# Loading k, q and v with one DMA per head pair instead of one per two head pairs

## The chip, the cores and the metric

One Trainium2 chip, one core of it. The metric is the time of one execution in microseconds on the device. Each profile is one execution taken by the hardware profiler. Runs carry a state: "slow" where a run lies over 1.5% above the fastest run of the same kernel, else "fast". With one core this is a label of spread, not of a die: the kernel before took 136.4 to 136.9 us in its first three runs.

## The reference, cut to what matters

Attention with a cosine weight (a feature map of relu times cos and sin, no softmax), whose output goes through a token mixer and a product with `w_out`:

```python
q_p = concat([relu(q) * cos, relu(q) * sin])      # also k_p; batch 8, heads 8, seq 576, head_dim 64
kv  = einsum('bhsf,bhsd->bhfd', k_p, v);  z = k_p.sum(axis=2)
x   = einsum('bhsf,bhfd->bhsd', q_p, kv) / (einsum('bhsf,bhf->bhs', q_p, z) + 1e-6)
# x: (8, 576, 512)
wq, wk = x @ w_q, x @ w_k
out = relu((wq @ wk.T / 8) @ x) @ w_out
```

All inputs and outputs are float32; q, k and v are 28 MB together and the output 9.4 MB.

## The kernel before

The kernel is one list of operations in a fixed order, each with its engine. Work goes by tile groups H = 0 to 15 (half a batch element, that is two head pairs). `LD` loads k, q or v of one group, `RK`, `CV` and `DQ` make bfloat16 of it on ScalarE, GpSimd or VectorE, `MK` multiplies k by cos and sin, `QK`, `NM`, `XT` and so on are TensorE's, and `ST` stores. All DMAs are issued by the sync engine, in the list's order.

```python
SPLIT = (0, 15)                      # groups whose loads come one head pair at a time
def part(H, s):
    return (s, s + 1) if H in SPLIT else (0, 2)

def LD(eng, pb, t, H, s):            # 54 of these; eng is the sync engine
    lo, hi = part(H, s)
    b, h = divmod(H, 2)
    eng.dma_start(raw[t][H % N_RAW][:, lo:hi, :],           # N_RAW = 5 buffers
                  srcs[t][b][:, 2 * h + lo:2 * h + hi, :])  # rows of 2,304 bytes
# ... (cut)
V.memset(warm, 1.0)
for _ in range(N_WARM):              # 14 products before the data comes
    T.matmul(bank1(7, 0, 2048, FP32), warm[:, 0:P], warm, start=True, stop=True)
```

## Time and profile before

| | before |
|---|---|
| time, first three runs | 136.85 us median (136.44 to 136.91) |
| span of the profiled execution | 136.3 us |
| busy: TensorE, VectorE, ScalarE, GpSimd | 77%, 73%, 58%, 47% |
| DMA queue of loads and stores, share of 16 engines' span | 82.0% |
| DMAs: whole loads, half loads, weights, stores | 42, 12, 3, 44 |

A busy share is an average over stages with different limits, so the digits by slice are what to read; the prediction shows them.

### The profile page before, as it was taken

The page shows a single profiled execution, that of the slowest core. Times are in us where ns is not written, and L with a number is a line of the kernel's source. Part 1 is how long each engine was busy: PE and PEld are TensorE (multiplying, and loading weights), DVE is VectorE, ACT ScalarE, POOL GpSimd, SP SyncE. Part 2 cuts the span into 40 slices and gives each one's busy share as a digit, 9 for nine tenths or more (in the row PEclk, how much of TensorE's full clock was granted, in tenths as well). Part 3 has the DMA queues.
Part 4 walks back from the last instruction along what each step waited for, and adds up shares of the span by engine and source line. Part 5 has one row for each costly group of instructions (what it writes and reads, how often), then busy time and mean ns, then how long its engine had stood idle before and what let it go on. Part 6 is the DMA issues. An engine that isn't in the chain of part 4 may idle for free.

```text
span 136.3 us, 5166 instructions
## 1 busy us (share of the span) xinstructions
PE 104.7 (77%) x2247; PEld 68.8 (50%) x2262; DVE 100.1 (73%) x180; ACT 78.9 (58%) x112; POOL 64.4 (47%) x56
## 2 busy tenths in 40 slices
PE   5932966497869859783899998999939999999600
PEld 2311955466555446553475585588514966444200
DVE  2147799988999998999279788999784697755000
ACT  7106131984878477953559957989344647434410
POOL 7635778358399947846584354434617010000000
PEclk9995599959999999999599999999995999999995
DMA  4999999999999999999999950029998461158984
GB/s 133 317 402 398 393 390 345 375 393 385 392 390 389 391 338 313 362 400 400 410 401 411 398 231 5 0 46 303 325 403 314 101 221 43 38 123 271 262 233 112
DMA packets 20070, 39.39 MB, mean 289 GB/s; under 512 B 2640, under 2 KB 2640, under 8 KB 20048
## 3 DMA queue, kind: packets, MB, share of 16 engines
q1 hardware_dynamic: 20048, 39.07, 82.0%
q8 instruction: 17, 0.28, 0.8%
q14 instruction: 5, 0.04, 0.1%
HBM read 29.62 MB, written 9.44 MB: 286 GB/s over the span
## 4 chain that ended last, share of the span: by engine, by line
PE 52%; DMA 18%; DVE 8%; issue 8%; SPq 5%; ACT 3%; POOL 1%; ACTq 0%
PE banks L400 19%; DMA vf<-in_v_dram 8%; DMA kf<-in_k_dram 7%; PE banks L279 7%; PE banks L330 6%; PE banks L247 6%; PE banks L256 4%; PE banks L313 4%; PE banks L375 3%; DMA out_dram<-osb 3%; DVE kp L219 3%; SPq L417 2%; PE banks L358 2%; SPq L195 2%; DVE xs L296 2%
## 5 line engine op out<-in xcount | busy, mean ns | idle before, releaser
L184 POOL TENSOR_SCALAR qd<-qf 128x2304 bf16<-128x2304 f32 (+1 forms) x18 | 35.3, 1964 | 13.7 <-DMA qf<-in_q_dram 10.0
L400 PE MATMUL banks<-wo_sb,mix 128*128 128x512 bf16 x129 | 35.2, 391 | 2.1 <-issue 1.6
L219 DVE TENSOR_TENSOR kp<-rk,cossin 128x2304 bf16<-128x2304 bf16 (+1 forms) x18 | 26.6, 1490 | 1.6 <-POOL rk L184 1.2
L266 DVE TENSOR_TENSOR qpt<-banks,cst 128x1152 bf16<-128x1152 bf16 x32 | 23.5, 746 | 4.7 <-PE banks L256 4.7
L174 ACT COPY osb<-banks 128x512 f32<-128x512 f32 x30 | 17.2, 589 | 14.4 <-PE banks L400 7.9
L296 DVE TENSOR_TENSOR xs<-banks,rec 128x640 bf16<-128x640 f32 x32 | 25.2, 810 | 0.2
L247 PE MATMUL banks<-vb,kp 64*128 64x65 bf16 x576 | 16.1, 197 | 9.3 <-ACT vb L174 4.5
L388 ACT ACTIVATE mix<-banks 128x640 bf16<-128x640 f32 (+1 forms) x26 | 16.8, 657 | 8.2 <-PE banks L375 8.0
L247 PEld LDWEIGHTS <-kp 64*128 64x128 bf16 x576 | 13.0, 99 | 13.7 <-DVE kp L219 6.8
L400 PEld LDWEIGHTS <-mix 128*128 128x128 bf16 x144 | 12.4, 99 | 14.2 <-issue 2.5
L279 PE MATMUL banks<-kvs,qpt 128*128 128x65 bf16 x320 | 15.8, 199 | 3.3 <-issue 1.7
L174 ACT COPY xT<-banks 128x1280 bf16<-128x1280 bf16 x11 | 13.4, 1227 | 8.0 <-PE banks L313 7.9
L279 PEld LDWEIGHTS <-qpt 128*128 128x128 bf16 x320 | 13.9, 101 | 5.5 <-DVE qpt L266 1.7
L256 PE MATMUL banks<-ident,qd 64*128 64x64 bf16 x576 | 15.1, 195 | 0.7 <-issue 0.7
L178 POOL TENSOR_SCALAR vb<-vf 128x1152 bf16<-128x1152 f32 (+1 forms) x8 | 10.0, 1256 | 11.5 <-DMA vf<-in_v_dram 8.6
L184 POOL TENSOR_SCALAR rk<-kf 128x1152 bf16<-128x1152 f32 (+1 forms) x8 | 10.1, 1267 | 10.3 <-DVE kp L219 4.9
L174 ACT CAST vb<-vf 128x1152 bf16<-128x1152 f32 (+1 forms) x10 | 11.1, 1108 | 5.4 <-DMA vf<-in_v_dram 5.4
L182 ACT ACTIVATE rk<-kf 128x1152 bf16<-128x1152 f32 (+1 forms) x9 | 10.0, 1111 | 7.2 <-DMA kf<-in_k_dram 7.2
L256 PEld LDWEIGHTS <-qd 64*128 64x128 bf16 x576 | 11.9, 98 | 0.8 <-issue 0.8
L176 DVE CAST kvs<-banks 128x130 bf16<-128x130 f32 x32 | 8.7, 279 | 4.7 <-PE banks L256 4.3
L330 PE MATMUL banks<-xT,wqk_sb 128*128 128x288 bf16 x64 | 10.2, 304 | 1.5 <-issue 1.5
L313 PE MATMUL banks<-ident,xs 64*128 64x64 bf16 x320 | 8.2, 199 | 3.8 <-issue 2.5
(50 smaller groups left out, 120.7 us busy)
## 6 DMA issues: line engine op xcount, KB each, us to landing
qf<-in_q_dram SPq DMA_DIRECT2D x14, 576.0 KB, 9.6
kf<-in_k_dram SPq DMA_DIRECT2D x14, 576.0 KB, 9.6
vf<-in_v_dram SPq DMA_DIRECT2D x14, 576.0 KB, 9.2
out_dram<-osb SPq DMA_DIRECT2D x28, 256.0 KB, 5.3
out_dram<-osb SPq DMA_DIRECT2D x16, 128.0 KB, 2.5
kf<-in_k_dram SPq DMA_DIRECT2D x4, 288.0 KB, 5.7
qf<-in_q_dram SPq DMA_DIRECT2D x4, 288.0 KB, 7.0
vf<-in_v_dram SPq DMA_DIRECT2D x4, 288.0 KB, 6.5
```

Of the source, the lines that this page charges most:

```text
L174: A.copy(dst, src)
L184: eng.tensor_scalar(dst, src, FMAX, 0.0, op0=ALU.min, op1=ALU.max)
L219: eng.tensor_mul(kp[H % N_KP][:, lo:hi], rk[H % N_RK][:, lo:hi].unsqueeze(3).to_broadcast([P, n, C9, 2, D]), cossin.unsqueeze(1).to_broadc ...
L247: T.matmul(kvp[:, hh, :], kp[H % N_KP][p0:p0 + 64, i, c, :, :], vb[H % N_VB][p0:p0 + 64, i, c, 0:D + 1], start=(c == 0), stop=(c == C9 - 1))
L256: T.transpose(qt[:, hh, c * D:(c + 1) * D], src, ident[p0:p0 + 64, p0:p0 + 64])
L266: eng.tensor_mul(qpt[g % N_QPT][:, :, 1:SLOTS, :], qk_views(at["QK", g])[0].rearrange("f h (c d) -> f h c d", c=C9), cst.unsqueeze(1).to_b ...
L279: T.matmul(nv[:, hh, u, :], qpt[g % N_QPT][:, hh, 2 * u:2 * u + 2, :], kvs[g % N_KV][:, hh, :], start=(u == 0), stop=(u == SC - 1 and not ...
L296: eng.tensor_tensor(xs[b % N_XS][:, :, 2 * pr:2 * pr + 2, :].rearrange("p u h d -> p h u d"), num_view(at["NM", g])[:, :, :, 0:D], rec[g % ...
L313: T.transpose(xv[:, r, i, u, :], xs[b % N_XS][p0:p0 + 64, u, 2 * hp:2 * hp + 2, :], ident[p0:p0 + 64, p0:p0 + 64])
L330: T.matmul(w[:, nh, :], wqk_sb[:, dmc, :], xT[b % N_XT][:, dmc, D + nh * HS:D + (nh + 1) * HS], start=(dmc == 0), stop=(dmc == NDM - 1))
L388: A.activation(dst, src, AF.Relu, scale=scale_moe)
L400: T.matmul(o, mix[b // 2 % N_MIX][:, dmc, base:base + P], wo_sb[:, dmc, :], start=(dmc == 0), stop=(dmc == NDM - 1))
```

## The change

Each load of a whole group becomes two DMAs, one per head pair, at the same place in the order. The intent is smaller pieces; no byte and no order changes.

```diff
     def LD(eng, pb, t, H, s):
         lo, hi = part(H, s)
         b, h = divmod(H, 2)
-        eng.dma_start(raw[t][H % N_RAW][:, lo:hi, :],
-                      srcs[t][b][:, 2 * h + lo:2 * h + hi, :])
+        for i in range(lo, hi):
+            eng.dma_start(raw[t][H % N_RAW][:, i, :], srcs[t][b][:, 2 * h + i, :])
```

## The prediction

> **What bounds the kernel now.** I read four views of the kernel before: the page, then the sync engine's queue in order of time, then its waits, then the waits of the compute engines on DMAs stage by stage.
>
> The page, part 2 (one digit for each 3.4 us):
>
> ```profile
> PE   5932966497869859783899998999939999999600
> ...
> DVE  2147799988999998999279788999784697755000
> ...
> DMA  4999999999999999999999950029998461158984
> GB/s 133 317 402 398 393 390 345 375 393 385 392 390 389 391 338 313 362 400 400 410 401 411 398 231 5 0 46 303 325 403 314 101 221 43 38 123 271 262 233 112
> ```
>
> The 16 DMA engines are full from 3 to 79 us at about 390 GB/s; nearly all of k, q and v arrive there. From about 65 us TensorE is full, the DMA engines are empty around 82 to 90 us, then comes a second, short load stage (to 106 us) and a tail of stores. So the first half is paced by bytes, with VectorE close behind, and the second half by TensorE. Splitting moves no bytes. It can only hurt through a cost per DMA, or through fewer bytes queued ahead.
>
> The sync engine issues all loads and stores in one order (start, duration):
>
> ```profile
> 0.73 0.40 SPq L195 DMA_DIRECT2D kf<-in_k_dram  x1
> ...
> 2.12 0.43 SPq L195 DMA_DIRECT2D qf<-in_q_dram  x1
> ...
> 8.28 0.38 SPq L195 DMA_DIRECT2D vf<-in_v_dram  x1
> 9.06 0.37 SPq L195 DMA_DIRECT2D kf<-in_k_dram  x1
> ...
> 40.91 1.26 SPq L195 DMA_DIRECT2D qf<-in_q_dram  x1
> 49.26 0.73 SPq L417 DMA_DIRECT2D out_dram<-osb  x1
> 50.03 0.58 SPq L195 DMA_DIRECT2D qf<-in_q_dram  x1
> 50.66 0.78 SPq L195 DMA_DIRECT2D vf<-in_v_dram  x1
> ...
> 89.78 0.47 SPq L417 DMA_DIRECT2D out_dram<-osb  x1
> ```
>
> Its waits (total, times, longest):
>
> ```profile
> SPq L417 <- DVE osb L176: 16.1, 2, 12.5
> SPq L417 <- ACT osb L174: 12.0, 5, 6.8
> ...
> SPq L195 <- DMA kf<-in_k_dram: 5.1, 5, 1.1
> ```
>
> The first issue (0.73) is a half load, 288 KB; the one at 2.12 is a whole one, 576 KB. They take 0.40 and 0.43 us: an issue costs the same whatever its size. Line L195's waits on a DMA that loads another tile are a depth limit: the trace's landing events use 8 semaphores, and at 8.28 us issue number 12 starts just after number 4 has landed (8.26); 9.06 follows 9.04, 10.53 follows 10.52. So at most 8 DMAs are in flight. Twice the queue stands long in front of a store whose data isn't computed (42.2 to 49.26, and 76 to 89.78 us), and loads queue up behind it.
>
> Loads just in time, 52 to 66 us:
>
> ```profile
> POOL qd L184 <- DMA qf<-in_q_dram: 3.5, 2, 2.7
> ...
> POOL vb L178 <- DMA vf<-in_v_dram: 2.6, 2, 1.9
> ```
>
> So GpSimd waits for landings in this stage, and a load that lands later there would be felt.
>
> [...] the first half load, alone, takes 3.0 us from issue to landing, 2.2 us more than its bytes need; behind other DMAs this vanishes: half loads land 0.76 and 0.75 us apart (13.52, 14.28, 15.03 us) and whole ones 1.48 to 1.50. [...] 294,912 bytes in 0.755 us are 391 GB/s, 589,824 in 1.50 us are 393. [...] 1,617 four-byte packets, 16 for each of 101 DMAs and one more.
>
> **The change part by part.** There are 54 loads. Twelve (tile groups 0 and 15) are half loads already. The other 42 become 84; 101 DMAs become 143. Rows of 2,304 bytes, bytes and order stay.
>
> 1. *Issues.* 42 more, at 0.37 to 0.47 us in a quiet stage and about 0.6 beside stores (50.03: 0.58), so 16 to 25 us more of the sync engine's time. In the saturated stage this lies beside transfer: a half load is issued every 0.45 us and drained every 0.75. At the start 288 KB per 0.46 us are 640 GB/s against some 390 drained. On the path: about 0.
>
> 2. *Completions.* [...] The mean four-byte packet in the trace takes 9.6 ns: 0.4 us in all, 0.3 us by the landing of tile group 10's q (30 whole loads until then). The landings say the same: two halves, 2 x 0.755, against 1.50 for a whole is 0.01 us per extra DMA. The load stage is saturated, so I take it in full as delay of landings at 50 to 60 us: +0.3 us.
>
> 3. *Depth.* Eight in flight were up to 4.7 MB, some 12 us of transfer; eight halves are 2.36 MB, 6.0 us. That still covers the 2.2 us of latency, if the queue keeps being issued. In front of the store at 42.2 us the kernel before stands 7 us with a backlog that lands until 52.75, so 3.5 us are left when it goes on. With halves the queue comes to the store later (around 47 us), because it waits for semaphores first, but at 49.26 the same bytes have been queued and the same 3.5 us are left. Depth is thus lost without cost: the order before each store is unchanged, and all before it is issued by then.
>
> 4. *Refill after that store.* Here issue rate counts. Before: nine DMAs between 49.26 and 55.7 us, about 3.9 MB, restore the backlog. After: five loads become ten, so some 14 issues of 0.65 us (duration plus gap) = 9.1 us for 9.9 us of transfer. The queue stays ahead by little. The kernel before already dips here: 338 and 313 GB/s in slices 15 and 16 against 390[...]. With 288 KB per 0.65 us (450 GB/s) refill is slower, and I allow a further loss of 0 to 0.7 us, middle 0.2. GpSimd waits for q's landing at 62.13 us, and TensorE has about 0.6 us of slack behind it, so maybe half of this arrives.
>
> 5. *Second load stage.* Issues at 90.3 to 94.8 us: three extra, some 1.5 us more issue time. These loads matter (tile group 14's relu on GpSimd starts at 98.08, its k landed at 97.91), and a ScalarE eviction at 100.67 us seems to wait for a store that landed at 100.57. But the landings are 4 to 8 us after their issues, so transfer, not issue, sets them: 0 to 0.3, middle 0.1.
>
> 6. *Waits of consumers.* ScalarE and GpSimd operations on a whole tile must wait for two semaphores instead of one. Such waits are separate instructions of 17 to 43 ns, run ahead when the engine is busy (gaps between GpSimd operations are -0.03 us with and without), and put an operation about 0.07 us later where it wakes on it. Much of this is off the path: +0.1 us at most.
>
> Nothing is gained: relu, cast and duplication work on whole tiles and wait for the later half, which lands when the whole did.
>
> Sum: 0.3 + 0.1 + 0.1 + 0.1 = 0.6 us as landings and waits are delayed; the second half is TensorE's, which absorbs part, so I put +0.4 us on 136.85: 137.2 us.
>
> **Rivals.** *The issue rate becomes the bound.* For: 143 issues; single issues beside stores of 1 to 1.7 us. Against: most of the long ones (1.2 to 3.7 us, 15 to 41 us) come with seven DMAs outstanding, where the queue has time. If issue takes 0.9 us each in stages 4 and 5, landings slip 2 to 3 us and the time is 139 to 140.
>
> *The shallower queue runs dry at the store waits.* For: half the bytes in flight. Against: step 3. If loads behind the first stop came 2 us late, about 138.5.
>
> *It gets faster.* [...] shorter backlogs let the instruction fetches of TensorE through sooner, and smaller completions free things earlier. For: several TensorE gaps of 1 to 2.5 us without a wait (49.82, 62.52 us) lie near fetches of 16 KB. Against: [...] the buffers come free as whole tiles. At best 135.5.
>
> *Timing luck.* The order is tuned to today's landings; a shift of 0.3 us can move which engine wakes first, either way by some 0.5 us.
>
> **Range and chances.** The terms add to between 0 and 1.5 us, with luck of half a microsecond either way, hence 136.2 to 138.8. Two per cent is 2.7 us; slower than 139.6 needs the first rival; faster than 134.1 has no mechanism. Chances: faster 0.02, same 0.89, slower 0.09.
>
> **What would show it.** Right: 42 more DMAs and the same rows; the DMA digits still 9 until about 79 us, GB/s near 390; half loads landing 0.73 to 0.76 us apart; sync-engine issues of 0.4 us with waits on DMAs in total longer; the store still issued near 49.3 and 90 us. Wrong: DMA digits of 7 or 8 between 48 and 62 us, issues back to back there with three or fewer outstanding, GpSimd's waits on q and v grown by over 2 us, or the store of 89.78 us more than 2 us later.

## More of the kernel before

Everything is unrolled: TensorE's stream has 2,262 weight loads and as many matrix products, which alternate, so 4,524 instructions.

One part of the page that neither the table nor the prediction takes up turns out to matter, the DMA queues of the kernel before (packets, MB, share):

```profile
q1 hardware_dynamic: 20048, 39.07, 82.0%
q8 instruction: 17, 0.28, 0.8%
```

The second queue carries instructions, not data: 17 packets of 16,384 bytes. If a packet holds 256 instructions (the stops found below are 256 apart), 17 of them are 4,352 instructions. Only TensorE's stream is of that size; the trace has under 250 instructions for each other engine.

## The result, and the profile after

The changed kernel takes 131.38 us (median of 4, 130.66 to 132.96) against 136.88 us (136.44 to 138.24) for the kernel before. The ratio is 0.9565, 95% interval 0.9474 to 0.9656. A ratio is the mean time of one kernel's fast runs over that of the other's of the same rounds, so not quite the ratio of the medians. The prediction, 137.2 us within 136.2 to 138.8, was wrong: the kernel is faster by over 4% here (a repeat on another chip, after_b below, gives 2.4% by fast runs and 3.5% by medians).

In the two traces TensorE's weight loads and all operations of VectorE, ScalarE and GpSimd are the same, one for one. Only the sync engine's instructions and the waits for loads differ.

The page of the changed kernel, part 2 (here one digit is 3.3 us):

```profile
PE   5811965599879899997999999899759999999500
...
DVE  3337789985999999999799899989485996764000
...
DMA  4999999999999999999999999069997653068985
GB/s 145 297 383 404 393 392 369 351 390 367 394 388 392 389 390 350 325 398 351 381 351 372 362 393 359 28 161 304 382 351 249 156 175 85 0 167 269 255 230 119
```

The DMA engines are as full as before and for longer (to 82 us instead of 79), at slightly less than before: 350 to 380 GB/s from 60 to 75 us, where the kernel before had 398 to 411. Load by load, what lands up to 60 us lands between 0.8 us sooner and 0.9 us later than before, and what lands from 62 to 82 us is 0.1 to 2.2 us later. So sooner arrival is not what gains 5 us. What is different is TensorE between 34 and 65 us, where the digits of before had a 3, a 5 and a 6 among them and the lowest is now 7.

The sync engine's queue of the changed kernel (start, duration):

```profile
0.73 0.38 SPq L196 DMA_DIRECT2D kf<-in_k_dram  x1
...
7.82 0.33 SPq L196 DMA_DIRECT2D qf<-in_q_dram  x1
8.54 0.33 SPq L196 DMA_DIRECT2D vf<-in_v_dram  x1
...
46.01 1.09 SPq L196 DMA_DIRECT2D qf<-in_q_dram  x2
48.71 0.73 SPq L417 DMA_DIRECT2D out_dram<-osb  x1
49.49 1.51 SPq L196 DMA_DIRECT2D qf<-in_q_dram  x2
...
84.88 0.47 SPq L417 DMA_DIRECT2D out_dram<-osb  x1
```

Around 8 us issues are now 0.72 us apart, about the time that a half load takes to drain (0.75 us). The queue reaches the first store's wait at 47.1 us instead of 42.2 and goes on at 48.71 us instead of 49.26. The store that left at 89.78 us leaves at 84.88: between these two stores 4.4 us are won.

Its waits (total, times, longest), and GpSimd's wait on loads between 52 and 66 us:

```profile
SPq L417 <- DVE osb L176: 10.3, 2, 5.7
SPq L196 <- DMA qf<-in_q_dram: 5.7, 14, 0.6
SPq L196 <- DMA vf<-in_v_dram: 5.6, 15, 0.4
SPq L196 <- DMA kf<-in_k_dram: 4.8, 12, 0.4
```

```profile
POOL qd L184 <- DMA qf<-in_q_dram: 4.6, 2, 3.5
```

GpSimd waits longer for q than before (4.6 against 3.5 us), as q of group 10 lands at 62.58 us instead of 62.13. Its wait for v in this stretch (2.6 us before) is gone. TensorE is 2.5 us ahead by then, although the loads in question landed no sooner. So who waited less? The waits of TensorE's weight loads, 27 to 66 us of before and 27 to 62 us of after:

```profile
PEld L313 <- issue: 3.4, 3, 2.6
PEld L330 <- issue: 1.7, 1, 1.7
...
PEld L283 <- issue: 1.2, 1, 1.2
...
PEld L247 <- DVE rec L289: 1.0, 1, 1.0
```

```profile
PEld L313 <- issue: 1.5, 2, 1.0
...
PEld L247 <- DVE rec L289: 1.0, 1, 1.0
...
PEld L330 <- issue: 0.3, 1, 0.3
```

"Issue" is time for which the profile shows no semaphore. These waits shrink or vanish, and the longest are single stops, most of them in the middle of a run of equal instructions. The last line of the first view is a wait of another kind, with a name: it is for VectorE, and it stays. TensorE's timeline at the longest stop, before and then after:

```profile
62.24 0.18 PEld L313 LDWEIGHTS <-xs 64*128 64x128 bf16 x7
65.06 0.26 PEld L313 LDWEIGHTS <-xs 64*128 64x128 bf16 x13 [2.63 <-issue]
```

```profile
59.75 0.18 PEld L313 LDWEIGHTS <-xs 64*128 64x128 bf16 x7
60.95 0.26 PEld L313 LDWEIGHTS <-xs 64*128 64x128 bf16 x13 [1.02 <-issue]
```

Seven of twenty transposes run, then TensorE stops for 2.63 us, then the other thirteen run. No data can be missing between the seventh and the eighth, for all twenty read the same tile. Counting from the start of TensorE's stream, the stop is before instruction 2,240. Two more stops of before are of this kind:

```profile
49.41 0.22 PEld L330 LDWEIGHTS <-wqk_sb 128*128 128x128 bf16 x2
51.29 0.22 PEld L330 LDWEIGHTS <-wqk_sb 128*128 128x128 bf16 x2 [1.66 <-issue]
```

```profile
56.94 0.22 PEld L279 LDWEIGHTS <-qpt 128*128 128x128 bf16 x5
58.31 0.10 PEld L283 LDWEIGHTS <-ones_t 128*128 128x128 bf16 x1 [1.16 <-issue]
```

They are before instructions 1,728 and 1,984. The three counts are 256 apart, as many instructions as the estimate above gives one packet of the instruction queue. With the packets' start times from the trace, the boundaries read as follows ("gap" is the time between the starts of the weight loads on both sides; "fetch" is the time from the crossing to the start of the next 16 KB packet; us). The gap at 1,472 is the named wait for VectorE just shown, not a wait for instructions:

```
            before                      after
count   crossed   gap   fetch      crossed   gap   fetch
  960     32.70  1.21   3.73         32.11  0.03    2.92
 1472     45.40  1.09   3.49         44.85  1.06    2.10
 1728     51.29  1.76   4.64         49.37  0.39    2.89
 1984     58.31  1.26   4.34         55.58  0.03    3.16
 2240     65.05  2.73   3.74         60.94  1.11    2.82
 3008     82.27  0.84   1.05         76.58  0.03    2.68
 3776     99.87  0.94   2.52         94.03  0.03    2.63
```

The arithmetic of one stop: before, TensorE crosses 1,984 at 58.31 us. The next packet starts 4.34 us later, takes 0.92 us, and TensorE goes on 1.48 us after its end, at 65.05, which is 6.74 us after the crossing. The 256 instructions between took 4.01 us. The difference, 2.73 us, is the stop. After, the same three terms are 3.16, 0.92 and 1.28 us, together 5.36, against 4.25 us of work: 1.11 us. Where the DMA engines are empty (count 3,264 of before, at 89.28 us) the packet starts 0.58 us after the crossing and there is no stop.

This holds beyond the one stop. The traces of the kernel before, of the changed kernel and of page_shift and page_shift_after (below; eight traces) have 35 stops over 0.3 us without a named wait at counts of 192 modulo 256 from 960 on. In all 35 TensorE goes on 1.2 to 1.6 us after the end of the packet. So the packet's landing ends them. At 1,472, in the six traces of the two kernels, TensorE goes on 1.7 to 2.7 us after it.

Theory 1, then: TensorE's instruction fetches wait behind the load bytes in flight. Both traces have at most 8 DMAs in flight (in before the landing events use 8 semaphores, and issue 12 starts at 8.28 us, just after number 4 has landed at 8.26), so by an estimate from their sizes halves put up to 2.4 MB ahead of a fetch instead of 4.7 MB. Theory 2: the smaller loads themselves help (landing in pieces, cheaper issues). Theory 3: luck of timing.

### The profile page after: what moved, and what is told of

Read it like the earlier page. It is cut to its first block, busy times and chain, and to the rows that moved or that the text cites.

```text
span 131.1 us, 5242 instructions
## 1 busy us (share of the span) xinstructions
PE 105.2 (80%) x2262; PEld 69.1 (53%) x2262; DVE 98.7 (75%) x180; ACT 79.1 (60%) x112; POOL 64.4 (49%) x56
## 2 busy tenths in 40 slices
DMA packets 20743, 39.39 MB, mean 300 GB/s; under 512 B 3313, under 2 KB 3313, under 8 KB 20721
## 4 chain that ended last, share of the span: by engine, by line
PE 43%; DVE 21%; DMA 13%; issue 7%; SPq 6%; ACT 5%; ACTq 0%; DVEq 0%
PE banks L400 12%; DMA out_dram<-osb 8%; DVE xs L296 7%; PE banks L247 7%; PE banks L256 5%; PE banks L279 5%; DVE kp L219 5%; PE banks L330 5%; DMA vf<-in_v_dram 5%; DVE qpt L266 4%; PE banks L313 3%; SPq L196 3%; SPq L417 3%; PE banks L375 3%; ACT vb L174 2%
## 5 line engine op out<-in xcount | busy, mean ns | idle before, releaser
L184 POOL TENSOR_SCALAR qd<-qf 128x2304 bf16<-128x2304 f32 (+1 forms) x18 | 37.0, 2058 | 11.9 <-DMA qf<-in_q_dram 8.1
L400 PE MATMUL banks<-wo_sb,mix 128*128 128x512 bf16 x144 | 36.6, 389 | 0.4 <-issue 0.4
L178 POOL TENSOR_SCALAR vb<-vf 128x1152 bf16<-128x1152 f32 (+1 forms) x8 | 9.1, 1144 | 12.5 <-DMA vf<-in_v_dram 8.4
L184 POOL TENSOR_SCALAR rk<-kf 128x1152 bf16<-128x1152 f32 (+1 forms) x8 | 9.3, 1161 | 7.0 <-DMA kf<-in_k_dram 5.1
L283 PE MATMUL banks<-eps_t,ones_t 128*128 128x5 bf16 x64 | 11.2, 175 | 0.0
L375 PE MATMUL banks<-wqk,kx 64*128 64x320 bf16 (+1 forms) x32 | 8.5, 293 | 2.8 <-ACT kx L174 2.2
```

The source lines that it names most:

```text
L184: eng.tensor_scalar(dst, src, FMAX, 0.0, op0=ALU.min, op1=ALU.max)
L375: T.matmul(m[:, r, :], kxs[b % N_KX][p0:p0 + 64, i * P:(i + 1) * P], w, start=True, stop=True)
L400: T.matmul(o, mix[b // 2 % N_MIX][:, dmc, base:base + P], wo_sb[:, dmc, :], start=(dmc == 0), stop=(dmc == NDM - 1))
```

## The experiments

Fifteen kernels ran in four jobs (a job is one batch of runs on one chip). Gaps are summed over all boundaries from count 960 on, less 0.03 us each, the normal distance. The sums take in the named wait at 1,472, which is 0.5 to 1.1 us in kernels of either kind.

**tiny1 and tiny2: fewer bytes in flight with whole loads.** The edit to the kernel before; tiny2 has `range(2)`:

```diff
         eng.dma_start(raw[t][H % N_RAW][:, lo:hi, :],
                       srcs[t][b][:, 2 * h + lo:2 * h + hi, :])
+        if hi - lo == 2:
+            for _ in range(1):
+                eng.dma_start(tiny[n_tiny[0] % 12], srcs[t][b][0:16, 2 * h, 0:1])
+                n_tiny[0] += 1
```

> Whole loads of 576 KB as before, but each followed by a load of 64 bytes on the same queue, so that the 8 DMAs in flight hold four whole loads: the same 2.4 MB as with halves, and the same 143 DMAs. Theory 1 (TensorE's instruction fetches of 16 KB wait behind the load bytes in flight): as the changed kernel, 131 to 133 us; the fetch after a crossing of a 256-instruction boundary starts 2 to 3.3 us later between 27 and 66 us (before: 3.5 to 4.6), and the gaps before boundaries 960, 1728, 1984 and 2240 shrink from 7.0 us to under 2.5 us. Theory 2 (the halves themselves: landing in smaller pieces, cheaper issues): as before, 136 to 138 us. Theory 3 (luck of timing, no system in it): anything, and fetch delays as before.

> As tiny1 with two small loads behind each whole load, so 2.7 whole loads (1.6 MB, some 4 us of transfer) are in flight, less than with halves. Theory 1: fetch delays fall further, to some 1.5 to 2.5 us, gaps at the boundaries under 1.5 us; 130 to 132 us unless the loads begin to run dry (then the GB/s falls below 370 in the load stage and the time goes up to 133 to 136). Theory 2: 136 to 139 us. Theory 3: anything.

Measured: tiny1 134.93 us (133.77 to 137.03), ratio 0.9758 [0.9614, 0.9901]; gaps 6.9 us. tiny2 147.83 us (147.16 to 151.52), ratio 1.0705 [1.0579, 1.0831]; gaps 1.2 us. So whole loads with fewer bytes in flight gain 2.4%, where halves gained 4.3% in the result above and 2.4% in the repeat (after_b). This speaks against theory 2 in its pure form, but the forecast of 131 to 133 us and of small gaps was too good. In tiny2 the gaps nearly vanish, and the loads run dry: fewer than three of them in flight bring some 300 GB/s. Its small gaps are no support for theory 1, though. The mean delay from crossing to packet is 3.0 us between 25 and 77.5 us (2.6 us without the crossing of 1,472, where the packet had started before it), where 1.5 to 2.5 us were forecast. TensorE, short of data, takes 7.0 us for 256 instructions there, which is longer than such a fetch. Depth has a price on both sides.

**split_late and split_early: halves in one part only.** The step is 1 where the condition holds, else the whole:

```diff
-        eng.dma_start(raw[t][H % N_RAW][:, lo:hi, :],
-                      srcs[t][b][:, 2 * h + lo:2 * h + hi, :])
+        step = 1 if H >= 8 else hi - lo          # split_early: H < 8
+        for i in range(lo, hi, step):
+            eng.dma_start(raw[t][H % N_RAW][:, i:i + step, :],
+                          srcs[t][b][:, 2 * h + i:2 * h + i + step, :])
```

> Only loads of tile groups 8 to 14 are made as halves (those issued from about 34 us). Theory 1: the gaps at boundaries 1728, 1984 and 2240 shrink (5.8 us before, 1.5 us with all halves), the one at 960 stays (1.2 us): 132 to 133.5 us. Theory 2 with the gain spread over all loads: half of it, about 134. Theory 3: anything.

> Only loads of tile groups 1 to 7 are made as halves. Theory 1: the gap at boundary 960 (1.2 us before) goes and landings up to 40 us may be 0.5 us earlier, the gaps at 1728, 1984 and 2240 stay: 135 to 136.5 us. Theory 2 with the gain spread over all loads: half of it, about 134. Theory 3: anything.

Measured: split_late 134.89 us (133.7 to 135.57), ratio 0.9787 [0.9643, 0.993], gaps 4.1 us. split_early 135.3 us (134.41 to 136.86), ratio 0.9791 [0.9659, 0.9923], gaps 8.9 us. The sum of the gaps went as theory 1 says: late halves remove most of it, early ones don't. At the one boundary that early halves should have cleared, 960, it went the other way: 0.86 us stayed with early halves (the fetch before it still took 3.56 us), and nothing was left with late ones (0.64 us or more with either in the repeats below). The times did not follow theory 1 either: each part gained about 2%, which is what "gain spread over all loads" had forecast. This is taken up again below.

**before_b and after_b: second traces.** No edit.

> The kernel before itself, for a second trace. Theory 1 (TensorE waits for its own instructions at every 256th, behind the loads): gaps at boundaries 960, 1728, 1984 and 2240 add to 5 us or more again, and the fetch starts 3.4 to 4.6 us after the crossing of the boundary before, between 27 and 66 us. Theory 3 (luck): gaps and delays elsewhere or gone.

> The changed kernel itself, for a second trace and a comparison beside the others. Theory 1: ratio 0.95 to 0.97, gaps at those four boundaries together under 3 us, fetch starts 2 to 3.3 us after a crossing. Theory 3: gaps and delays as in the kernel before in one of the traces.

Measured: before_b 138.84 us (2 runs), gaps 9.4 us. after_b 132.31 us (130.47 to 134.21), ratio 0.9763 [0.9609, 0.9917], gaps 3.7 us. The ratio misses its forecast of 0.95 to 0.97; by medians (137.14 us for the kernel before in this job) it is 0.965. The kernel before stops at 1,728 and 2,240 again, this time not at 960 and 1,984, and at 2,496 and 3,008 instead. So the forecast of 5 us at the four named boundaries failed (3.3 us): which boundary costs what varies from run to run, and the sum over all does not.

**page_shift and page_shift_after: more instructions ahead of the work.** The same edit to the kernel before and to the changed one:

```diff
-    for _ in range(N_WARM):
-        T.matmul(bank1(7, 0, 2048, FP32), warm[:, 0:P], warm, start=True, stop=True)
+    for _ in range(N_WARM + 64):
+        T.matmul(bank1(7, 0, 368, FP32), warm[:, 0:P], warm[:, 0:92], start=True, stop=True)
```

> The kernel before with 78 warm-up products of 92 columns in place of 14 of 512, which is 64 pairs (128 TensorE instructions) more before the real work and about as long. Theory 1: the long gaps stay at counts of 192 modulo 256 from the start of TensorE's stream, so they come 128 instructions earlier in the real work: before what were instructions 1600, 1856, 2112, 2368 (new counts 1728, 1984, 2240, 2496), and the gaps before the old 1728, 1984 and 2240 are gone; time within 2% of before. If the gaps belong to the work (data, banks), they stay at the old places, at new counts 1856, 2112, 2368.

> The same 64 pairs added to the changed kernel. Theory 1: again gaps only at counts of 192 modulo 256, smaller than in page_shift (together under 3 us between counts 900 and 2600), and 3 to 5% faster than page_shift. Theory 3 (the changed kernel happened to fit): no gain over page_shift.

Measured: page_shift 137.3 us (135.85, 138.74), gaps 8.0 us; page_shift_after 133.81 us (132.75, 134.87), gaps 5.1 us. That is 2.5% faster, where 3 to 5% were forecast, and its gaps between 900 and 2,600 are 3.5 us instead of under 3; the one at 1,216 (2.29 us) is no shorter than with whole loads. In page_shift the stops are before the new counts 960 (0.53 us), 1,216 (2.02), 2,496 (2.64), 3,008 (1.54) and 4,288 (1.16), all of them 192 modulo 256. The old places, at new counts 1,856, 2,112 and 2,368, have none. The largest one, in the timeline of page_shift:

```profile
67.01 0.15 PEld L279 LDWEIGHTS <-qpt 128*128 128x128 bf16 x3
69.70 0.12 PEld L279 LDWEIGHTS <-qpt 128*128 128x128 bf16 x2 [2.54 <-issue]
```

Now another group of instructions is cut, after its third of five. The stops belong to the count and not to the work, and they end with the packet's landing: they are waits for instructions. The named wait moved with the work instead, from 1,472 to 1,600 (0.52 us). Not every "issue" gap is such a stop: page_shift has 0.97 and 0.96 us before 2,044 and 2,144, which are no boundaries, and what they wait for stays open. The expectation named 1,728 to 2,496; only 2,496 of these four came, which again is the spread over boundaries.

**after_c, half_tiny and after_noeps.** half_tiny puts the 64-byte load of tiny1 behind the two halves of each load of the changed kernel; after_noeps is the changed kernel with `EPS_PE = False`.

```diff
         for i in range(lo, hi):
             eng.dma_start(raw[t][H % N_RAW][:, i, :], srcs[t][b][:, 2 * h + i, :])
+        if hi - lo == 2:
+            eng.dma_start(tiny[n_tiny[0] % 12], srcs[t][b][0:16, 2 * h, 0:1])
+            n_tiny[0] += 1
```

> The changed kernel again, as the yardstick for the two below on the same chip: 0.95 to 0.98 of the kernel before; gaps before the 256-instruction boundaries, all from count 900 on, 3 to 4 us together (3.2 and 3.9 in the two traces so far; kernel before 9.9 and 9.7).

> The changed kernel with one load of 64 bytes behind the two halves of each load, so that 5.3 halves (1.6 MB, 4 us) are in flight in place of 8. In the traces so far the fetch delay follows the backlog alone (mean 2.6 us at 4.5 to 5.5 us of backlog, 2.1 to 2.5 at 3 to 4.5, 3.7 at over 7, whole loads or halves alike). Theory 1 (backlog): delays of about 2.2 us between 27 and 72 us, boundary gaps from count 900 on under 3 us; if the DMA engines stay full (380 GB/s or more to 60 us), 0.98 to 1.0 of the changed kernel; if they run dry as with two small loads behind a whole load, the time goes up by 3 to 8 us although the gaps are small. If the size of the load counted and not the backlog, delays stay at 2.7 us.

> The changed kernel with the small constant of the denominator added by VectorE (32 more operations of some 0.2 us) in place of 64 matrix products, so 128 TensorE instructions of 4,524 fewer: half a fetch less, and boundaries that fall at other places. Theory 1: gaps still only at counts of 192 modulo 256, at other work; the time changes by what VectorE's 6 us more cost in its full stages: 0.99 to 1.03 of the changed kernel. No other theory has a forecast.

Measured: after_c 133.96 us (129.83 to 136.4; one run of four was labelled fast, so there is no ratio), gaps 2.9 us. half_tiny 144.07 us (142.81 to 144.8), ratio 1.0421 [1.0314, 1.0528], gaps 1.7 us. after_noeps 134.87 us (134.52 to 135.89), ratio 0.9777 [0.9687, 0.9867], so it gains nothing over the changed kernel; its gaps are 3.1 us, and the largest, 2.03 us, is at count 2,240, which in this stream is other work.

half_tiny shows the other side. Stretches from 27 to 66 us, half_tiny and then the changed kernel (stretch, length, busy time of each engine, granted clock, DMA share, GB/s):

```profile
27.00:66.00 39.00, 30.50 (x722) 21.39 (x728) 32.11 (x52) 26.87 (x39) 20.54 (x14) 0.90 0.91 299
```

```profile
27.00:66.00 39.00, 35.31 (x870) 24.62 (x865) 35.93 (x61) 30.02 (x43) 26.51 (x16) 0.94 1.03 376
```

Five halves in flight bring 299 instead of 376 GB/s, at a DMA share of 0.91 instead of 1.03, and every compute engine is less busy in this stretch (TensorE 30.50 instead of 35.31 us). GpSimd waits 6.6 us for k and 5.1 us for v there, ScalarE 6.0 us for k. The test between backlog and size of a DMA did not decide: the mean delay between 27 and 72 us is 2.6 us, or 2.3 without the crossing of 1,472, where 2.2 us spoke for backlog and 2.7 for size. Of the depths tried eight halves are the best; no version that I tried beats the changed kernel.

**Second traces of the parts: split_early_b, split_late_b, tiny1_b, before_c.** No new edits.

> split_early again. If the gaps are the whole cause, they add to 7.5 to 9.5 us again and the time is 0.98 to 1.0 of before; if the early halves help in another way (0.97 to 0.98 of before with gaps over 8 us), landings before 45 us must be earlier than in before_c by 1 us or more, or slow clock in the second half must be rarer.

> split_late again. If the gaps are the whole cause: together 3.5 to 5 us, and 0.96 to 0.975 of before; otherwise 0.975 to 0.985 as in the first job.

> tiny1 again. If the bytes in flight decide: gaps together 4 to 7 us, less than with whole loads alone, with delays between crossing and fetch of 2 to 3.3 us where the backlog is under 5.5 us; 0.97 to 0.98 of before (part of the gain is lost to loads that land later: 316 to 323 GB/s around 22 us in the first trace). If only halves do it: gaps of 8 us or more.

> The kernel before, for a third trace: gaps before 256-instruction boundaries together 8 to 10 us, delays between crossing and fetch 3.4 to 3.8 us on average between 26 and 76 us; ratio 0.99 to 1.01.

Measured: split_early_b 135.74 us (133.38 to 138.36, one fast run, no ratio), gaps 8.4 us. split_late_b 133.69 us (131.34 to 135.86), ratio 0.9731 [0.9413, 1.0048], gaps 4.5 us. tiny1_b 135.04 us (131.23 to 137.55, one fast run, no ratio), gaps 4.5 us. before_c 137.15 us (136.59 to 138.03), ratio 1.0099 [0.9982, 1.0215], gaps 10.2 us. The gaps of split_early_b, split_late_b and tiny1_b are as forecast, those of before_c just above (8 to 10 us).

**All traces together.** "Last" is the start of TensorE's last weight loads (count 4,522), "fetch" the mean time from crossing to packet between 25 and 77.5 us, "slow clock" the time between 34 and 112 us in which TensorE had half of its clock (us):

```
kernel            gaps           fetch          last              slow clock
whole loads
  before          9.6            3.74           127.7             6.8
  before_b        9.4            3.48           129.5             6.8
  before_c        10.2           3.79           127.6             0
halves
  after           2.9            2.67           122.6             3.4
  after_b         3.7            2.71           120.2             0
  after_c         2.9            2.54           122.8             3.4
tiny1, tiny1_b    6.9, 4.5       3.17, 3.05     126.8, 125.3      3.4, 3.4
split_late, _b    4.1, 4.5       3.05, 3.22     123.9, 125.5      3.4, 0
split_early, _b   8.9, 8.4       3.42, 3.16     123.8, 124.7      0, 3.4
```

For whole loads against halves this closes. The mean of the gaps falls from 9.7 to 3.2 us, by 6.6 (by 6.3 without the named wait at 1,472), and the last weight loads come 6.4 us earlier (128.3 to 121.9). At count 3,006, the end of the first load stage, TensorE is at 79.5 to 82.2 us with whole loads and at 74.5 to 77.3 us with halves; take the stops at boundaries out of each trace (all but 1,472), and it is 74.4 to 75.4 against 73.3 to 76.0 us, which is level. Each group has two slow traces and a fast one. The fast pair alone, before_c and after_b, neither with slow clock between 34 and 112 us, says the same: 6.5 us less in gaps and 7.4 us earlier, of which 1.3 us are there by count 1,470 already.

Whether bytes in flight or the size of a DMA sets the delay, I read from all crossings before 112 us, sorted by backlog (from the crossing until the last DMA whose issue had ended by then has landed). The mean delay to the packet, with the number of crossings; whole loads include page_shift, halves page_shift_after:

```
backlog, us      whole         halves        tiny1, tiny1_b
3 to 4.5         2.92 (6)      2.06 (19)     2.51 (10)
4.5 to 5.5       2.78 (5)      2.61 (22)     2.53 (9)
5.5 to 7         3.63 (14)     3.00 (14)     3.26 (8)
over 7           3.66 (28)     3.90 (5)      3.88 (3)
```

From the first row to the last the delay grows with the backlog in all three (2.92 to 3.66, 2.06 to 3.90 and 2.51 to 3.88 us); for whole loads it is the same in the last two rows (3.63 and 3.66 us). Whole loads sit mostly in the last two rows (42 of 53), halves in the first two (41 of 60). At equal backlog whole loads wait 0.2 to 0.9 us longer than halves in the first three rows, and not in the last. (If a DMA counts from the start of its issue, the four differences are -0.1, 0.4, 0.6 and 0.0 us.) So the backlog is the larger part. That the size of a DMA adds something is not excluded.

## Why the prediction was wrong

What held:

- **Issues.** In the quiet stage a half load costs the sync engine mostly 0.33 to 0.45 us (predicted 0.37 to 0.47), beside the stores from 48 to 62 us 0.53 us in the median (predicted 0.6), and the issue rate never became the bound. The prediction had an issue cost the same whatever its size; in the quiet stage a half takes 0.33 us and a whole 0.37.
- **Completions.** Halves land 0.75 us apart (9.28, 10.03, 10.78 us), and the page counts 20,743 packets against 20,070, which is 42 times 16 and one more.
- **Backlog at the store.** The queue comes to the first store at 47.1 us ("around 47 us") and leaves it with 3.9 us of backlog (the last load before it lands at 52.60 us, the store is issued at 48.71). The DMA engines did not run dry (digits of 9 up to 82 us).
- **Later landings.** In the first load stage q of group 10 lands 0.45 us later and q of group 13 1.25 us later (78.60 to 79.85). The sum of +0.6 us for landings was of the right sign and size, and it did not matter.

None of the signs named for being wrong came up (the DMA digits stay 9 between 48 and 62 us): they all watch the loads, and none watches TensorE.

What failed is a sentence of step 3, "Depth is thus lost without cost", together with the answer given to the third rival. The prediction had seen TensorE's gaps at 49.82 and 62.52 us and the 16 KB fetches beside them, and put them aside without a number of the trace. The trace had the numbers: in the stage of the loads, 27 to 66 us, a fetch started 3.5 to 4.6 us after its boundary was crossed, and in the empty stage around 89 us 0.6 us. Depth did not come for nothing; it had a cost that the change took away: 6.3 us of stops in the mean of three traces each, 5.5 us in the medians of the result. "Faster than 134.1 has no mechanism" fell with it, and so did the "at best 135.5" given to that rival, which had named the mechanism and was mis-sized. (By the prediction's own terms the range is 136.4 to 138.9 us, not 136.2 to 138.8; this changes nothing.)

A second sentence failed in the same way. "From about 65 us TensorE is full" and "the first half is paced by bytes, with VectorE close behind" took the digits of TensorE before 65 us for waits on data. The changed kernel shows that much of it was TensorE waiting for its own instructions: its digits there rise although the loads land no sooner.

What is shown and what is not:

- That the stops are at counts of TensorE's own stream that are 256 apart is shown: with 128 more instructions ahead of the work, page_shift has them at counts of 192 modulo 256 again (2.64 us at 2,496), at other work.
- That whole loads and halves differ by these stops is shown by the sums above, for the two whole kernels. With page_shift and page_shift_after, and the named wait at 1,472 left out, the stops are 8.0 to 9.3 us of some 136 in four traces with whole loads, and 1.8 to 5.1 us in four with halves.
- That bytes in flight cause the delay is supported by tiny1, which has whole loads and less delay (3.1 against 3.7 us), and by the table of backlogs; tiny2 and half_tiny, with fewer bytes still, add no clear support. From crossing to packet a fetch took 0.6 to 1.2 us where nothing was left to land (three traces of the kernel before) and 3.7 us on average with over 7 us of backlog; then came 0.9 to 1.8 us for the packet. Why the wait is some 3 us longer with a backlog is open. Whether it waits for the end of a DMA the traces can't tell, since they don't say which DMA engine a packet is on.
- The parts are not settled. split_late's gaps fell by 5.4 us on average, but its second load stage lost some of this in one of two traces: from count 3,006 to 3,400 it took 12.8 and 10.7 us, against 9.6 to 10.7 for whole loads. split_early kept its gaps, and is nevertheless 3.5 to 4.5 us earlier at the last weight loads than whole loads. So boundary stops do not seem to be all that the size of the loads changes. Of the ways named for it before the run, slow clock in the second half was no rarer than in before_c or after_b. Earlier landings were there in part: loads that land at 20 to 26 us do so 1.3 us sooner in split_early_b than in before_c, but those at 38 to 45 us only 0.4 us, and the first trace of before is itself 0.8 us sooner than before_c at 20 to 26 us. Why early halves gain about 2% stays open, and so does how the two parts come to add up so well.

The mean granted clock does not explain the result. It is 0.925 over twelve runs of the changed kernel and 0.920 over 34 runs of the kernel before (in the four jobs of experiments), with mean times of 132.5 and 138.0 us. Within the changed kernel the time follows the clock, by about 0.7 us for 0.01; an estimate from these numbers for a clock higher by 0.005 is 0.4 us.

## What to carry to other kernels

Where TensorE's stream is long and unrolled and a deep queue of loads runs beside it, look at its "issue" gaps: see whether they cut a run of equal instructions, lie 256 instructions apart and end soon after a packet of the instruction queue. All 35 stops in eight traces here ended 1.2 to 1.6 us after one: TensorE was waiting for its own program. Then try fewer bytes in flight, as long as the DMA engines stay full. Here halves with 2.4 MB in flight (376 GB/s from 27 to 66 us) beat whole loads with 4.7 MB (379 GB/s) by 4% (2.4% in the repeat, fast runs), and 1.6 MB (299 GB/s in half_tiny) lost 4 to 7% against the kernel before. Smaller DMAs cost no bandwidth here: in a full queue 288 KB and 576 KB drained at 391 and 393 GB/s. In a prediction, a gap without a named wait needs a cause with a number, not an argument.
